# Token rows of six experts and of fifteen second-MLP tiles transposed through DRAM and VectorE instead of TensorE

## The chip, the cores and the metric

The kernel runs on one core of a Trainium2 chip. Its time is the device time of one execution in microseconds; the number compared is the median of several runs. A separate execution was recorded by the hardware profiler; times along the trace count from its first instruction.

## The reference

Three stages on 2304 tokens (4 batches of 576) of width 512. All inputs are float32.

```
q_s = softmax(q, over the 64 columns of a head)     # 8 heads
k_s = softmax(k, over the 576 rows)
x   = q_s @ (k_s^T @ v), heads side by side         # 2304 x 512

noisy = x @ w_gate + log1p(exp(x @ w_noise)) * noise   # 8 experts
top-2 of noisy per token, softmax over the two
x   = sum over the two experts e of weight * (relu(x @ w1[e]) @ w2[e])   # 512 -> 1024 -> 512

h   = x @ w_in                                       # 512 -> 1024
s   = h * softmax(h)
x   = (s - mean(s)) / sqrt(var(s) + 1e-6) * g_ln @ w_out   # 1024 -> 512
```

## The kernel before, in words

Matrix products that feed values into the two MLPs are done in three passes: each float32 operand is split into a high part (fp32r, made by a ScalarE copy) and a low part (the difference, made by VectorE), and TensorE adds high x high, high x low and low x high.

The order of the work is written out by hand; each engine takes its instructions in that order, and waits are placed where tiles are handed over or buffers are reused. DMAs are issued by SP, except the gathers, which POOL issues. SP issues in program order too: an issue that waits holds back all behind it.

**Attention and expert 0** follow a written-out list (ORDER) and take until about 180 us.

**Experts 1 to 7** are one loop. Each expert has room for 640 tokens, five tiles of 128. For an expert e, eight steps `mm1(e, m)` (L758) make a 128-row block of the hidden layer each; their results go through ScalarE (Relu, high part hh, L762) and VectorE (low part hl, L763), from two psum buffers in turn, so the matmuls of step m need the hl of step m - 2. In steps m < 4 the weights W2 of e are split and the weights W1 of e + 1 are loaded (`load_w1`, L148, one DMA of 512 KB). In steps m < 5 the token rows of e + 1 are gathered by POOL into a ring of five row tiles (`gather_x`, L727). From m = 3 on, one step of a background generator runs in each m: `decode_all`. Its first step only issues the loads of decode tiles 0 and 1 (`load_f64`, L195); after that a tile takes four steps of VectorE work (L203 to L218), the last of which also issues the store (L219) and the load of the tile two ahead. This generator makes w_in and w_out readable for the second MLP through DRAM copies win32 and wout32. Three decode buffers per tile come from a ring of four.

Then come five turns `mm2(e, a)` (L794), one per token tile, 24 matmuls each. In each turn the tile a of the next expert is transposed before them: `xt_tile` calls `transpose_split` (L734 four TensorE transposes into psum, L736 ScalarE copy to the high part, L737 VectorE subtraction to the low part). A turn also evacuates its result (L796, VectorE and ScalarE by turns) and stores it, does a decode step, splits a quarter of the next W1 and loads a quarter of the next W2.

**The second MLP** goes over 18 tiles. `gather_y` fetches the two expert results of a tile, `combine` weighs and adds them (L824, L825), `x2_trans` transposes the 128x512 result on TensorE and splits it (L734, L736, L737), `h_in` does 48 matmuls (L842), `solu` takes the row maximum (L851), the exponential (L854), and the normalised product d (L855 to L862), `rstd` the variance (L870 to L880). For tiles 2 to 15 d already goes through DRAM: `d_write`, then `d_read` with four DMAs that put 32-row blocks in place, and `d_back`: one VectorE transpose in blocks of 32x32 (L898), a ScalarE copy (L901), a VectorE subtraction (L902). Other tiles transpose d on TensorE (`d_trans`). `o_out` does 24 matmuls (L925). One turn i of the final loop has `h_in(i)`, then d back for i - 2, x2 for i + 1, `solu(i)`, `combine(i + 3)`, `rstd(i - 1)` and `o_out(i - 3)` (`o_out(i - 2)` in turns 2 and 3, none in turn 4).

A transpose in blocks of 32x32 leaves the 512 contraction rows in another order over the partitions than a full transpose; the weights must be loaded in the same order, as `load_w2` already does for w_out.

Of the kernel before, what the change touches and what calls it, by code (L numbers as in the profile page):

```python
# [8 lines left out]
F32 = mybir.dt.float32  # L9
F32R = mybir.dt.float32r  # L10
F16 = mybir.dt.float16
I32 = mybir.dt.int32
U32 = mybir.dt.uint32
# [12 lines left out]
NA = 5  # L26
# [27 lines left out]

NP = 2

ORDER = """
F:100011101100000000100000000000101111 lk:0 lq:0 lkl:0 lk:1 kr:0 kmt:0 qm:0 lvl:0 km:0:0 klt:0 kl:0 km:0:1 kb:0
lk:2 kr:1 qs:0 lv:0 rz:0 ks:0 kmt:1 ksl:0 qe:0 kr:2 km:1:0 T:0 kmt:2 rz:1 km:1:1 C:0 kb:1 lkl:1 rz:2 T:1 km:2:0
# [25 lines left out]
def attn_moe_kernel(ctx: ExitStack, tc: tile.TileContext, q, k, v, w_gate, w_noise, noise,  # L85
# [11 lines left out]
    def slot(tag, shape, dt, name):  # L97
        return sb.tile(shape, dt, tag=tag, name=name)

    def ring(*tags):  # L100
        state = [-1]

        def take(shape, dt, name):
            state[0] = (state[0] + 1) % len(tags)
            return slot(tags[state[0]], shape, dt, name)
        return take

    new_raw = ring("R2", "R3", "R0", "R1")
    new_row = ring("S0", "S2", "S4", "S1", "S3")
    new_out = ring("S9", "S8", "S10")  # L110
    new_s2 = ring("S5", "S6", "S7", "S11")
    psA = ctx.enter_context(tc.tile_pool(name="psA", bufs=2, space=PSUM))
    psB = ctx.enter_context(tc.tile_pool(name="psB", bufs=2, space=PSUM))
# [4 lines left out]
    tab = dram.tile([OVT * 128, 2], I32, name="tab")  # L118
    win32 = dram.tile([DM, FF], F32, name="win32")
    wout32 = dram.tile([FF, DM], F32, name="wout32")  # L120
    dd = {t: dram.tile([128, FF], F32, name=f"dd{t}") for t in range(NP, NC - 2)}

    def bank_t():
# [20 lines left out]

    def load_w1(e, j):
        t = new_raw([128, KD, 256], F32, "raw")
        src = win32 if e == E else w1[e]
        SP.dma_start(out=t, in_=src[:, 256 * j:256 * j + 256].rearrange("(k p) f -> p k f", p=128))  # L148
        raw[1, e, j] = t

    def load_w2(e, j):
# [46 lines left out]
    def decode(i):  # L198
        _, dst, rs, c0 = dec_src(i)
        t = d64.pop(i).rearrange("p (c w) -> p c w", w=2)  # L200
        lw, hw = t[:, :, 0], t[:, :, 1]
        a, b, c = (new_s2([128, 512], U32, f"dec{j}") for j in range(3))
        V.tensor_scalar(b, hw, 3, 0x3FFFFFF8, op0=OP.logical_shift_left, op1=OP.bitwise_and)  # L203
        V.scalar_tensor_tensor(a, hw, 0xC0000000, b, op0=OP.bitwise_and, op1=OP.bitwise_or)
        V.scalar_tensor_tensor(a, lw, 29, a, op0=OP.logical_shift_right, op1=OP.bitwise_or)
        yield

        V.tensor_scalar(b, lw, 0x1FFFFFFF, 6, op0=OP.bitwise_and, op1=OP.logical_shift_right)
        V.tensor_scalar(c, a, 0xFF800000, None, op0=OP.bitwise_and)
        V.tensor_tensor(b, b, c, op=OP.bitwise_or)  # L210
        yield
        af, bf, cf = (x.bitcast(F32) for x in (a, b, c))
        V.tensor_sub(bf, bf, cf)
        V.scalar_tensor_tensor(af, bf, 2.0 ** -23, af, op0=OP.mult, op1=OP.add)
        yield

        V.tensor_scalar(c, hw, 20, 0x7FF, op0=OP.logical_shift_right, op1=OP.bitwise_and)
        V.scalar_tensor_tensor(af, c, 896.5, af, op0=OP.is_ge, op1=OP.mult)  # L218
        SP.dma_start(out=dst[rs, c0:c0 + 512], in_=af)  # L219
# [501 lines left out]
    xg = {}  # L721

    def gather_x(e, a):
        t = new_row([128, DM], F32, "xg")
        c = E * a + e
        first = e == 0 and a < TA
        P.indirect_dma_start(out=t, out_offset=None, in_=xd[0:NRA, :] if first else xd, in_offset=bass.IndirectOffsetOnAxis(  # L727
            ap=idxA[:, a:a + 1] if first else idx[:, c:c + 1], axis=0))
        xg[e, a] = t

    def transpose_split(t, hi, lo):
        ps = bank_t()
        for kk in range(KD):
            T.transpose(ps[:, 128 * kk:128 * kk + 128], t[:, 128 * kk:128 * kk + 128], ident)  # L734
        pv = ps.rearrange("p (k t) -> p k t", k=KD)
        A.copy(hi, pv)  # L736
        V.tensor_sub(lo, pv, hi)  # L737
# [3 lines left out]
    def xt_tile(e, a):  # L741
        if a == 0:
            XT[e] = (slot("XH", [128, KD, CAP], F32R, "xh"), slot("XL", [128, KD, CAP], F32R, "xl"))
        hi, lo = XT[e]
        transpose_split(xg.pop((e, a)), hi[:, :, 128 * a:128 * a + 128], lo[:, :, 128 * a:128 * a + 128])

    hT = {}

# [72 lines left out]
    def combine(t):  # L821
        a, b = yg.pop((t, 0)), yg.pop((t, 1))
        c = col_of(t)
        A.activation(out=a, in_=a, func=AF.Copy, scale=gw[:, c, 0:1])  # L824
        V.scalar_tensor_tensor(a, b, gw[:, c, 1:2], a, op0=OP.mult, op1=OP.add)  # L825
        x2r[t] = a

    def x2_trans(t):
        a = x2r.pop(t)
# [14 lines left out]
                                 stop=(kk == KD - 1 and s == 2), skip_group_check=True)  # L844
        hb[t] = pa

    def solu(t):
        pa = hb.pop(t)
        c = col[:, t]
        pf = pa.rearrange("p n f -> p (n f)")  # L850
        V.reduce_max(c[:, 0:1], pf, axis=AX, negate=True)  # L851
        ed = new_ed([128, 2, FF], F32, "ed")
        e, d = ed[:, 0], ed[:, 1]
        A.activation(out=e, in_=pf, func=AF.Exp, bias=c[:, 0:1], accum_out=c[:, 1:2])  # L854
        V.tensor_scalar(c[:, 2:3], c[:, 1:2], 1e-9, None, op0=OP.add)  # L855
        V.reciprocal(c[:, 2:3], c[:, 2:3])
        V.scalar_tensor_tensor(d, pf, c[:, 2:3], e, op0=OP.mult, op1=OP.mult, accum_out=c[:, 3:4])  # L857
        V.tensor_scalar(c[:, 4:5], c[:, 3:4], -1.0 / FF, None, op0=OP.mult)
        if NP <= t < NC - 2:
            V.tensor_scalar(d, d, c[:, 4:5], None, op0=OP.add)  # L860
        else:
            V.tensor_scalar(e.rearrange("p (k g c) -> p g k c", g=4, k=KF), d.rearrange(  # L862
                "p (g k c) -> p g k c", g=4, k=KF), c[:, 4:5], None, op0=OP.add)
            e, d = d, e
        rsd[t] = e, d, c[:, 7:8]
# [23 lines left out]
    def d_read(t):  # L889
        x = dq[t] = new_dq([128, 2, FF], F32, "dq")  # L890
        for g in range(4):
            SP.dma_start(out=x[32 * g:32 * g + 32, 0].rearrange("i (b f) -> i b f", b=4),
                         in_=dd[t].rearrange("(b i) f -> i b f", i=32)[:, :, 256 * g:256 * g + 256])

    def d_back(t):
        x = dq.pop(t)
        xt = x[:, 1].rearrange("p (k b i) -> p k b i", k=KF, b=4)
        V.transpose(xt.rearrange("p k b i -> p b k i"), x[:, 0].rearrange("p (b k c) -> p b k c", b=4, k=KF))  # L898
        xt = xt.rearrange("p k b i -> p k (b i)")
        dt = new_dT([128, 2, KF, 128], F32R, "dT")  # L900
        A.copy(dt[:, 0], xt)  # L901
        V.tensor_sub(dt[:, 1], xt, dt[:, 0])  # L902
        dT[t] = (dt[:, 0], dt[:, 1])

    def d_trans(t):
        d = rsd[t][1]
# [222 lines left out]
    for e in range(1, E):  # L1129
        for m in range(KF):  # L1130
            mm1(e, m)
            if m < 4:
                split_w2(e, m)
                load_w1(e + 1, m)
            if e + 1 < E and m < NA:
                gather_x(e + 1, m)
            if m >= 3:
                next(bg, None)
            if e == 2 and m == 5:
                pair_gates()  # L1140
                count_overflow()
        if stop:
            return
        for a in range(NA):
            if e + 1 < E:
                xt_tile(e + 1, a)
            mm2(e, a)
            if e < E - 1:
                next(bg, None)
                if a < 4:  # L1150
                    split_w1(e + 1, a)
                    load_w2(e + 1, a)
                continue
            gather_y(a)
            if a < 2:
                for j in (2 * a, 2 * a + 1):
                    split_w1(E, j)
                    load_w2(E, j)
            elif a == 2:
                next(bg, None)  # L1160
                combine(0)
                split_w2(E, 0)
            elif a == 3:
                x2_trans(0)
                combine(1)
                split_w2(E, 1)
# [7 lines left out]
    for i in range(NC + 3):  # L1174
        if i < NC:
            h_in(i)
        if i == 1:
            d_trans(0)
        if NP <= i - 1 < NC - 2:
            d_read(i - 1)  # L1180
        if NP <= i - 2 < NC - 2:
            d_back(i - 2)
        if 2 <= i < NC - 1:
            x2_trans(i + 1)
        if i < NC:
            solu(i)
        if NP <= i < NC - 2:
            d_write(i)
        if i == 0:
            x2_trans(2)  # L1190
        if i < NC - 3:
            combine(i + 3)
        if i == 1:
            split_w2(E, 3)
        if 1 <= i <= NC:
            rstd(i - 1)
        if 2 <= i < 2 + NP:
            o_out(i - 2)
        if i >= 3 + NP:
            o_out(i - 3)  # L1200
        if i in (NP, NC - 1, NC):
            d_trans(i - 1)
        if i + 5 < NC:
            gather_y(i + 5)

# [30 lines left out]
```

## Time and profile before

| | us |
|---|---|
| median of 3 runs | 807.34 (806.57 to 809.58) |
| profiled execution | 807.68 |
| its span, first to last instruction | 806.0 |
| TensorE (matmul) busy | 758.2, 94% of the span |
| VectorE busy | 501.2, 62% |
| ScalarE busy | 293.8, 36% |
| GpSimd busy | 144.6, 18% |
| DMA moved | 119.98 MB, mean 149 GB/s |
| mean granted TensorE clock | 0.982 |

In the rows below PE is TensorE's matmuls, DVE VectorE, ACT ScalarE, POOL GpSimd and SPq the issue queue of SyncE. Matmul records overlap their neighbours: how far apart they start counts, not how long one is shown. An arrow names what ended a wait.

### The profile page before, as it was taken

Reading aid. Unit: us, or ns where it says so; the run is one execution under the profiler, and the core shown is the slowest. Engines: PE = TensorE matmul, PEld = TensorE weight load, DVE = VectorE, ACT = ScalarE, POOL = GpSimd, SP = SyncE. Lnnn points to the kernel's source line nnn. Section 1 sums busy time; section 2 is a strip of 40 time slices with the busy share of each in tenths; the row PEclk is TensorE's granted clock in tenths of the full one; section 3 lists DMA queues with packets and bytes.
Section 4 is the critical chain, followed back from the end, with each engine's and each line's share of the span. In section 5 each row is a group of like instructions: output and inputs, shape, how many; then the busy total and the mean of one; then the engine's idle time right before and its main releaser. Section 6 shows DMA issues by size and latency. Waiting matters only on the chain. (4 is left out here: it accounts for less than half of the span.)

```text
span 806.0 us, 12480 instructions
## 1 busy us (share of the span) xinstructions
PE 758.2 (94%) x4934; PEld 684.0 (85%) x4934; DVE 501.2 (62%) x884; ACT 293.8 (36%) x486; POOL 144.6 (18%) x130
## 2 busy tenths in 40 slices
PE   2877869999999999999999999999999999999997
PEld 1777867989789889889899899899898899989985
DVE  6998773334656656556556646546457767767661
ACT  1656531323223323223223232232345354444451
POOL 3684564020110110110200100000342111100000
PEclk9998888999999999999999999999999999999999
DMA  9973444265363454454543552432844545553311
GB/s 274 278 236 119 145 157 139 75 205 157 119 195 107 139 173 144 157 166 136 169 132 121 182 180 94 157 108 76 231 124 146 169 145 158 157 157 131 114 44 39
DMA packets 81534, 119.98 MB, mean 149 GB/s; under 512 B 14912, under 2 KB 52800, under 8 KB 81472
## 3 DMA queue, kind: packets, MB, share of 16 engines
q1 hardware_dynamic: 75392, 99.22, 38.6%
q0 software_dynamic: 6080, 19.93, 9.1%
q8 instruction: 39, 0.64, 0.3%
q14 instruction: 23, 0.19, 0.1%
HBM read 87.67 MB, written 31.46 MB: 148 GB/s over the span
## 5 line engine op out<-in xcount | busy, mean ns | idle before, releaser
L758 PE MATMUL a<-xh,w1h 128*128 128x320 f32 x448 | 138.5, 309 | 1.2 <-DVE hl L763 1.2
L758 PE MATMUL a<-xl,w1h 128*128 128x320 f32 x448 | 138.4, 309 | 0.0
L758 PE MATMUL a<-xh,w1l 128*128 128x320 f32 x448 | 138.3, 309 | 0.0
L794 PE MATMUL b<-w2h,hh 128*128 128x512 f32 x320 | 128.7, 402 | 0.0
L794 PE MATMUL b<-w2h,hl 128*128 128x512 f32 x320 | 126.7, 396 | 0.0
L794 PE MATMUL b<-w2l,hh 128*128 128x512 f32 x320 | 126.3, 395 | 0.0
L762 ACT ACTIVATE hh<-a 128x640 fp32r<-128x640 f32 x56 | 39.6, 707 | 159.8 <-PE a L758 159.8
L727 POOL DMA_INDIRECT xg<-xd,idx x38 | 40.7, 1071 | 304.1 <-PE t L734 294.3
L763 DVE SCALAR_TENSOR_TENSOR hl<-a,hh 128x640 fp32r<-128x640 f32 x56 | 46.1, 824 | 65.0 <-ACT hh L762 64.9
L758 PEld LDWEIGHTS a<-xh,w1h 128*128 128x128 f32 x448 | 84.2, 188 | 1.8 <-DVE hl L763 1.4
L758 PEld LDWEIGHTS a<-xl,w1h 128*128 128x128 f32 x448 | 84.1, 188 | 0.4
L758 PEld LDWEIGHTS a<-xh,w1l 128*128 128x128 f32 x448 | 84.2, 188 | 0.0
L817 POOL DMA_INDIRECT yg<-yd,posi x36 | 35.0, 973 | 208.6 <-DVE w1l L164 100.1
L794 PEld LDWEIGHTS b<-w2h,hl 128*128 128x128 f32 x320 | 60.0, 187 | 13.9
L794 PEld LDWEIGHTS b<-w2l,hh 128*128 128x128 f32 x320 | 60.2, 188 | 13.0
L794 PEld LDWEIGHTS b<-w2h,hh 128*128 128x128 f32 x320 | 60.2, 188 | 12.6
L164 DVE TENSOR_TENSOR w1l<-raw,w1h 128x1024 fp32r<-128x1024 f32 x32 | 38.9, 1222 | 33.4 <-ACT w1h L163 33.4
L842 PE MATMUL a<-w1h,x2h 128*128 128x256 f32 x288 | 57.5, 281 | 1.2 <-ACT x2h L736 0.7
L842 PE MATMUL a<-w1h,x2l 128*128 128x256 f32 x288 | 57.0, 279 | 0.0
L842 PE MATMUL a<-w1l,x2h 128*128 128x256 f32 x288 | 56.8, 278 | 0.0
L796 DVE COPY yo<-b 128x512 f32<-128x512 f32 x24 | 16.6, 692 | 64.2 <-PE b L794 64.2
L925 PE MATMUL b<-w2x,dT 128*128 128x512 f32 x216 | 54.3, 400 | 0.0
(209 smaller groups left out, 1399.3 us busy)
## 6 DMA issues: line engine op xcount, KB each, us to landing
raw<-in_moe_w_dram SPq DMA_DIRECT2D x64, 512.0 KB, 3.7
yd<-yo SPq DMA_DIRECT2D x40, 256.0 KB, 2.0
dd<-ed SPq DMA_DIRECT2D x14, 512.0 KB, 2.6
dq<-dd SPq DMA_DIRECT2D x56, 128.0 KB, 3.8
k<-in_k_dram SPq DMA_DIRECT2D x4, 1024.0 KB, 8.0
q<-in_q_dram SPq DMA_DIRECT2D x4, 1024.0 KB, 8.0
v<-in_v_dram SPq DMA_DIRECT2D x4, 1024.0 KB, 10.6
xd<-xr SPq DMA_DIRECT2D x8, 512.0 KB, 2.6
```

Of the source, the lines that this page charges most:

```text
L164: (pick_engine(20 + j, P, V) if e == 0 else V).tensor_sub(W1l[j], t, W1h[j])
L727: P.indirect_dma_start(out=t, out_offset=None, in_=xd[0:NRA, :] if first else xd, in_offset=bass.IndirectOffsetOnAxis(ap=idxA[:, a:a + 1] ...
L758: T.matmul(pa[:, n, 0:HC], lhsT=a, rhs=b, start=(kk == 0 and s == 0), stop=(kk == KD - 1 and s == 2))
L762: A.activation(out=h2, in_=pa[:, :, 0:HC], func=AF.Relu)
L763: V.scalar_tensor_tensor(l2, pa[:, :, 0:HC], 0.0, h2, op0=OP.max, op1=OP.subtract)
L794: T.matmul(pb, lhsT=x, rhs=y, start=(kk == 0 and s == 0), stop=(kk == KF - 1 and s == 2))
L796: (A.copy if a % 2 else V.tensor_copy)(t, pb)
L817: P.indirect_dma_start(out=r, out_offset=None, in_=yd[0:n, :], in_offset=bass.IndirectOffsetOnAxis(ap=posi[:, c, j:j + 1], axis=0))
L842: T.matmul(pa[:, n, 256 * c:256 * c + 256], lhsT=x[:, kk, :], rhs=w[2 * n + c][:, kk, :], start=(kk == 0 and s == 0 and c == 0), stop=(kk ...
L925: T.matmul(pb, lhsT=x[:, kk, :], rhs=w, start=(kk == 0 and s == 0), stop=(kk == KF - 1 and s == 2))
```

## The change

Token rows of experts 2 to 7 (EQ = 2) are gathered into a ring of three hop tiles, written to DRAM and read back by four DMAs of 128 runs of 512 bytes per 32 partitions; VectorE transposes them in 32x32 blocks, ScalarE copies the high part and VectorE subtracts for the low part. The weights W1 of experts 2 to 7 and of the second MLP are loaded in four pieces in the matching order of rows. In the second MLP tiles 3 to 17 go the same way; tiles 0 to 2 are copied once into the matching order by ScalarE and still transposed by TensorE. The decode buffers have fixed places: the result alternates between two tiles, the two others are one each. The low parts of d and of x2 move behind the row maximum, where the exponential runs on ScalarE; the VectorE transposes move to the end of a turn.

```diff
--- before.py
+++ after.py
@@ -53,6 +53,8 @@
     return [(0, 128, (2 * j + c // R) * S + c % R, R)]
 
 NP = 2
+
+EQ = 2
 
 ORDER = """
 F:100011101100000000100000000000101111 lk:0 lq:0 lkl:0 lk:1 kr:0 kmt:0 qm:0 lvl:0 km:0:0 klt:0 kl:0 km:0:1 kb:0
@@ -108,6 +110,7 @@
     new_raw = ring("R2", "R3", "R0", "R1")
     new_row = ring("S0", "S2", "S4", "S1", "S3")
     new_out = ring("S9", "S8", "S10")
+    new_hop = ring("RH0", "RH1", "RH2")
     new_s2 = ring("S5", "S6", "S7", "S11")
     psA = ctx.enter_context(tc.tile_pool(name="psA", bufs=2, space=PSUM))
     psB = ctx.enter_context(tc.tile_pool(name="psB", bufs=2, space=PSUM))
@@ -118,6 +121,8 @@
     tab = dram.tile([OVT * 128, 2], I32, name="tab")
     win32 = dram.tile([DM, FF], F32, name="win32")
     wout32 = dram.tile([FF, DM], F32, name="wout32")
+    xx = {t: dram.tile([128, DM], F32, name=f"xx{t}") for t in range(3, NC)}
+    xs_d = {(e, a): dram.tile([128, DM], F32, name=f"xs{e}_{a}") for e in range(EQ, E) for a in range(NA)}
     dd = {t: dram.tile([128, FF], F32, name=f"dd{t}") for t in range(NP, NC - 2)}
 
     def bank_t():
@@ -144,8 +149,12 @@
 
     def load_w1(e, j):
         t = new_raw([128, KD, 256], F32, "raw")
-        src = win32 if e == E else w1[e]
-        SP.dma_start(out=t, in_=src[:, 256 * j:256 * j + 256].rearrange("(k p) f -> p k f", p=128))
+        src = (win32 if e == E else w1[e])[:, 256 * j:256 * j + 256]
+        if e < EQ:
+            SP.dma_start(out=t, in_=src.rearrange("(k p) f -> p k f", p=128))
+        else:
+            for g in range(4):
+                SP.dma_start(out=t[32 * g:32 * g + 32], in_=src[128 * g:128 * g + 128].rearrange("(k c) f -> c k f", c=32))
         raw[1, e, j] = t
 
     def load_w2(e, j):
@@ -199,7 +208,7 @@
         _, dst, rs, c0 = dec_src(i)
         t = d64.pop(i).rearrange("p (c w) -> p c w", w=2)
         lw, hw = t[:, :, 0], t[:, :, 1]
-        a, b, c = (new_s2([128, 512], U32, f"dec{j}") for j in range(3))
+        a, b, c = (slot(tag, [128, 512], U32, f"dec{j}") for j, tag in enumerate((("S5", "S6")[i % 2], "S7", "S11")))
         V.tensor_scalar(b, hw, 3, 0x3FFFFFF8, op0=OP.logical_shift_left, op1=OP.bitwise_and)
         V.scalar_tensor_tensor(a, hw, 0xC0000000, b, op0=OP.bitwise_and, op1=OP.bitwise_or)
         V.scalar_tensor_tensor(a, lw, 29, a, op0=OP.logical_shift_right, op1=OP.bitwise_or)
@@ -721,12 +730,22 @@
     xg = {}
 
     def gather_x(e, a):
-        t = new_row([128, DM], F32, "xg")
         c = E * a + e
+        t = (new_row if e < EQ else new_hop)([128, DM], F32, "xg")
         first = e == 0 and a < TA
         P.indirect_dma_start(out=t, out_offset=None, in_=xd[0:NRA, :] if first else xd, in_offset=bass.IndirectOffsetOnAxis(
             ap=idxA[:, a:a + 1] if first else idx[:, c:c + 1], axis=0))
         xg[e, a] = t
+
+    def write_x(e, a):
+        SP.dma_start(out=xs_d[e, a], in_=xg[e, a])
+
+    def read_x(e, a):
+
+        t = xg[e, a] = new_row([128, DM], F32, "xg")
+        for g in range(4):
+            SP.dma_start(out=t[32 * g:32 * g + 32].rearrange("i (b f) -> i b f", b=4),
+                         in_=xs_d[e, a].rearrange("(b i) f -> i b f", i=32)[:, :, 128 * g:128 * g + 128])
 
     def transpose_split(t, hi, lo):
         ps = bank_t()
@@ -741,8 +760,16 @@
     def xt_tile(e, a):
         if a == 0:
             XT[e] = (slot("XH", [128, KD, CAP], F32R, "xh"), slot("XL", [128, KD, CAP], F32R, "xl"))
-        hi, lo = XT[e]
-        transpose_split(xg.pop((e, a)), hi[:, :, 128 * a:128 * a + 128], lo[:, :, 128 * a:128 * a + 128])
+        hi, lo = (x[:, :, 128 * a:128 * a + 128] for x in XT[e])
+        t = xg.pop((e, a))
+        if e < EQ:
+            transpose_split(t, hi, lo)
+            return
+        x = slot(("S12", "Gt")[a % 2], [128, KD, 4, 32], F32, "xt")
+        V.transpose(x.rearrange("p k b i -> p b k i"), t.rearrange("p (b k c) -> p b k c", b=4, k=KD))
+        x = x.rearrange("p k b i -> p k (b i)")
+        A.copy(hi, x)
+        V.tensor_sub(lo, x, hi)
 
     hT = {}
 
@@ -823,7 +850,32 @@
         c = col_of(t)
         A.activation(out=a, in_=a, func=AF.Copy, scale=gw[:, c, 0:1])
         V.scalar_tensor_tensor(a, b, gw[:, c, 1:2], a, op0=OP.mult, op1=OP.add)
-        x2r[t] = a
+        if t in xx:
+            SP.dma_start(out=xx[t], in_=a)
+            return
+        p = x2r[t] = slot(f"RH{t}", [128, DM], F32, "x2p")
+        A.copy(p.rearrange("p (k g c) -> p g k c", g=4, k=KD), a.rearrange("p (g k c) -> p g k c", g=4, k=KD))
+
+    def x2_read(t):
+        x = x2r[t] = new_raw([128, 2, DM], F32, "xq")
+        for g in range(4):
+            SP.dma_start(out=x[32 * g:32 * g + 32, 0].rearrange("i (b f) -> i b f", b=4),
+                         in_=xx[t].rearrange("(b i) f -> i b f", i=32)[:, :, 128 * g:128 * g + 128])
+
+    def x2_turn(t):
+        x = x2r.pop(t)
+        hi = new_s2([128, KD, 128], F32R, "x2h")
+        lo = new_s2([128, KD, 128], F32R, "x2l")
+        xt = x[:, 1].rearrange("p (k b i) -> p k b i", k=KD, b=4)
+        V.transpose(xt.rearrange("p k b i -> p b k i"), x[:, 0].rearrange("p (b k c) -> p b k c", b=4, k=KD))
+        xt = xt.rearrange("p k b i -> p k (b i)")
+        A.copy(hi, xt)
+        x2T[t] = (hi, lo, xt)
+
+    def x2_low(t):
+        hi, lo, xt = x2T[t]
+        V.tensor_sub(lo, xt, hi)
+        x2T[t] = (hi, lo)
 
     def x2_trans(t):
         a = x2r.pop(t)
@@ -844,14 +896,19 @@
                                  stop=(kk == KD - 1 and s == 2), skip_group_check=True)
         hb[t] = pa
 
-    def solu(t):
-        pa = hb.pop(t)
+    def solu_max(t):
+        pa = hb[t]
         c = col[:, t]
         pf = pa.rearrange("p n f -> p (n f)")
         V.reduce_max(c[:, 0:1], pf, axis=AX, negate=True)
         ed = new_ed([128, 2, FF], F32, "ed")
         e, d = ed[:, 0], ed[:, 1]
         A.activation(out=e, in_=pf, func=AF.Exp, bias=c[:, 0:1], accum_out=c[:, 1:2])
+        hb[t] = pf, e, d
+
+    def solu(t):
+        pf, e, d = hb.pop(t)
+        c = col[:, t]
         V.tensor_scalar(c[:, 2:3], c[:, 1:2], 1e-9, None, op0=OP.add)
         V.reciprocal(c[:, 2:3], c[:, 2:3])
         V.scalar_tensor_tensor(d, pf, c[:, 2:3], e, op0=OP.mult, op1=OP.mult, accum_out=c[:, 3:4])
@@ -892,15 +949,19 @@
             SP.dma_start(out=x[32 * g:32 * g + 32, 0].rearrange("i (b f) -> i b f", b=4),
                          in_=dd[t].rearrange("(b i) f -> i b f", i=32)[:, :, 256 * g:256 * g + 256])
 
-    def d_back(t):
+    def d_turn(t):
         x = dq.pop(t)
         xt = x[:, 1].rearrange("p (k b i) -> p k b i", k=KF, b=4)
         V.transpose(xt.rearrange("p k b i -> p b k i"), x[:, 0].rearrange("p (b k c) -> p b k c", b=4, k=KF))
         xt = xt.rearrange("p k b i -> p k (b i)")
         dt = new_dT([128, 2, KF, 128], F32R, "dT")
         A.copy(dt[:, 0], xt)
-        V.tensor_sub(dt[:, 1], xt, dt[:, 0])
-        dT[t] = (dt[:, 0], dt[:, 1])
+        dT[t] = (dt[:, 0], dt[:, 1], xt)
+
+    def d_low(t):
+        hi, lo, xt = dT[t]
+        V.tensor_sub(lo, xt, hi)
+        dT[t] = (hi, lo)
 
     def d_trans(t):
         d = rsd[t][1]
@@ -1134,6 +1195,11 @@
                 load_w1(e + 1, m)
             if e + 1 < E and m < NA:
                 gather_x(e + 1, m)
+            if EQ <= e + 1 < E:
+                if 1 <= m < NA + 1:
+                    write_x(e + 1, m - 1)
+                if 3 <= m:
+                    read_x(e + 1, m - 3)
             if m >= 3:
                 next(bg, None)
             if e == 2 and m == 5:
@@ -1178,10 +1244,14 @@
             d_trans(0)
         if NP <= i - 1 < NC - 2:
             d_read(i - 1)
+        if 1 <= i < NC - 2:
+            x2_read(i + 2)
+        if i < NC:
+            solu_max(i)
         if NP <= i - 2 < NC - 2:
-            d_back(i - 2)
+            d_low(i - 2)
         if 2 <= i < NC - 1:
-            x2_trans(i + 1)
+            x2_low(i + 1)
         if i < NC:
             solu(i)
         if NP <= i < NC - 2:
@@ -1200,6 +1270,10 @@
             o_out(i - 3)
         if i in (NP, NC - 1, NC):
             d_trans(i - 1)
+        if NP <= i - 1 < NC - 2:
+            d_turn(i - 1)
+        if 1 <= i < NC - 2:
+            x2_turn(i + 2)
         if i + 5 < NC:
             gather_y(i + 5)
```

## Rows read from the trace of the kernel before

**Rows 1.** Busy time by stretch: us, then PE, PEld, DVE, ACT, POOL; clock, DMA, GB/s.
```profile
300.00:400.00 100.00, 100.00 (x580) 91.19 (x579) 60.36 (x84) 30.96 (x42) 8.77 (x8) 1.00 0.46 146
680.00:740.00 60.00, 60.00 (x399) 54.69 (x399) 43.61 (x88) 28.88 (x56) 5.67 (x6) 1.00 0.46 140
```

**Rows 2.** Waits of PE after 200 us: us in total, times, longest.
```profile
PE a L758 <- DVE hl L763: 1.2, 1, 1.2
```

**Rows 3.** Timeline around two turns of expert stages: start us, length us.
```profile
406.31 0.60 PE L734 MATMUL t<-ident,xg 128*128 128x128 f32 x4
...
406.98 0.39 PE L794 MATMUL b<-w2l,hh 128*128 128x512 f32 x1
407.20 0.39 PE L794 MATMUL b<-w2h,hl 128*128 128x512 f32 x1
...
412.33 0.31 PE L758 MATMUL a<-xh,w1h 128*128 128x320 f32 x1
...
409.22 0.69 DVE L737 TENSOR_TENSOR xl<-t,xh 128x512 fp32r<-128x512 f32 x1
```

**Rows 4.** The chain that ended last, at the second MLP's start: start us, length us.
```profile
618.47 0.66 PE t L734 x4
...
624.67 5.57 PE a L842 x48
...
630.70 0.59 ACT x2h L736
...
631.34 6.16 PE a L842 x48
637.50 0.44 PE t L734 x4
```

**Rows 5.** VectorE by line, 640 to 760 us: busy us, mean ns, idle before.
```profile
L898 DVE STREAM_TRANSPOSE dq<-dq 128x1024 f32<-128x1024 f32 x11 | 13.7, 1246 | 0.6 <-issue 0.4
L902 DVE TENSOR_TENSOR dT<-dq,dT 128x1024 fp32r<-128x1024 f32 x11 | 13.5, 1226 | 12.3 <-ACT dT L901 12.3
...
L737 DVE TENSOR_TENSOR x2l<-t,x2h 128x512 fp32r<-128x512 f32 x11 | 7.5, 684 | 0.0
...
L855 DVE TENSOR_SCALAR col<-col 128x1 f32<-128x1 f32 x11 | 1.7, 154 | 14.0 <-ACT ed L854 14.0
```

**Rows 6.** Timeline of VectorE at the second MLP's start.
```profile
618.33 0.68 DVE L916 TENSOR_TENSOR dT<-t,dT 128x512 fp32r<-128x512 f32 x1
...
620.38 1.22 DVE L851 TENSOR_REDUCE col<-a 128x1 f32<-128x1024 f32 x1
...
627.34 0.16 DVE L880 TENSOR_TENSOR col<-col 128x1 f32<-128x1 f32 x1
```

**Rows 7.** Timeline of DMA issues on SP: the first decode loads, one weight load, one d_read.
```profile
194.90 0.97 SPq L195 DMA_DIRECT2D f<-in_moe_w_in_dram  x2
...
397.31 0.38 SPq L154 DMA_DIRECT2D raw<-in_moe_w_dram  x1
...
673.92 1.75 SPq L892 DMA_DIRECT2D dq<-dd  x4
```

**Rows 8.** Timeline of VectorE in expert 1: the first decode step and what follows.
```profile
200.59 0.43 DVE L203 TENSOR_SCALAR dec<-f 128x512 uint32<-128x512 uint32 x1 [3.95 <-DMA f<-in_moe_w_in_dram]
...
202.39 0.82 DVE L763 SCALAR_TENSOR_TENSOR hl<-a,hh 128x640 fp32r<-128x640 f32 x1
```

**Rows 9.** TensorE before 130 us by stretch: us, PE busy, granted clock, DMA, GB/s.
```profile
114.60:118.20 3.60, 2.02 (x26) 1.00 0.35 86
118.30:121.70 3.40, 0.13 (x6) 0.89 0.00 0
121.70:127.80 6.10, 6.09 (x38) 0.50 0.01 3
```

**Rows 10.** DMA issues of the second MLP: count, KB each, median us to landing.
```profile
dd<-ed SPq DMA_DIRECT2D x14, 512.0 KB, 2.6
dq<-dd SPq DMA_DIRECT2D x56, 128.0 KB, 3.8
```

## The prediction

> **What bounds the kernel now.** I read the busy time by stretch first. In an expert stretch (300 to 400 us) and in the second MLP (680 to 740 us) TensorE is busy for all of it at a granted clock of 1.00, while VectorE stands at 60% and 73% and the DMA engines at 46% [rows 1]. The reader is to see that no other engine is near its limit there. Next come the waits that end idle time of TensorE after 200 us: the largest is 1.2 us, before a matmul of L758, released by VectorE [rows 2]; three more, under 1 us each, lie at the start of the second MLP [rows 4]. So from 200 us on the time is the sum of what TensorE executes, and an instruction taken off it is worth its own length, as long as nothing new is late.
>
> **The change part by part.**
>
> Transposes of experts 2 to 7. Six experts of five tiles lose four TensorE transposes each: 30 groups. In the timeline a group starts at 406.31 and the second matmul after it at 406.98; matmuls there follow each other every 0.23 (406.98 to 407.20). A group thus takes 0.67 - 0.23 = 0.44 us [rows 3]. 30 x 0.44 = 13.2 us go.
>
> What takes their place is a gather into a hop tile, one write to DRAM, four reads, one VectorE transpose, a ScalarE copy and a VectorE subtraction. The transpose of 128x512 is not in the trace. Bounds: 0.62 (half of the 1246 ns for 128x1024) and 1.25 (all of it); I take 0.65, near the half, because the 1024-wide subtraction and the 512-wide one (1226 and 684 ns) scale so [rows 5]. This is hidden if the last tile is ready when the next expert's first matmul starts. Before, the last low part ended at 409.91 and the matmuls of L758 began at 412.33 [rows 3], 2.4 us later. The new order adds a transpose (0.65) and a wait for ScalarE's copy (0.59, the x2h copy of [rows 4]) behind the same VectorE work, and the matmul comes 0.44 earlier: about 0.7 us remain, 0.1 with a transpose of 1.25. The first half of the matmuls needs only columns of the first three tiles, which is further cover. I cost it at nothing; without cover it would be up to 6 x 1 us.
>
> The Trainium skill ("VectorE: DVE Perf Modes", section "Rules for kernel authors") speaks against this exchange: for a 128x128 transpose it says to use TensorE if PSUM will do as destination. By that rule these groups would stay and this gain would be zero. The rows that make TensorE the only full engine decide here.
>
> SP in expert 1. This is the price I expect. SP issues in program order, and the first two decode loads (L195) sit at m = 3 of expert 1, now behind new issues. The W1 load of that step becomes four pieces: four issues take 1.75, as those of d do, against 0.38 for one weight load, +1.37. The write of tile 2 adds 0.38 and the four reads of tile 0 add 1.75 [rows 7]. Together +3.5 us; from below, if issues take less, +2.5, and from above +4.5 with more traffic ahead. Before, the load was issued at 194.90 and VectorE waited for it until 200.59, with the hl operation of L763 queued behind the decode step, at 202.39 [rows 7, 8]. TensorE's 1.2 us wait is this very wait: its next psum buffer is freed by that hl. So the late load goes straight onto the path: +3.4 us, and TensorE then stands idle for 1.2 + 3.4 = 4.6 us. The trace shows what such a gap does: TensorE was nearly idle from 118.3 to 121.7, and from 121.7 to 127.8 the granted clock was 0.50 (the 1.2 GHz level); a stretch of 3.6 us from 114.6 on, in which it was busy for 2.0, kept 1.00 [rows 9]. Half speed over 6.1 us costs about 3.0; where the low stretch ends sooner, 1.5. I take 2.5. Together +5.9 us, once. Later decode loads are issued two decodes ahead of their use and keep their cover.
>
> The Trainium skill ("DMA: Bandwidth & Descriptors", section "Issuing engines are not separate DMA queues") calls the sequencer's time to initiate a DMA usually small relative to the DMA itself. Here four issues take 1.75 us and the load some 5.7. Taken as negligible, the 3.5 us vanish and the sum is 5.9 better; that is the second rival.
>
> Two decode tiles. They take away VectorE waits for decode stores. No wait of TensorE hangs on those: nothing gained, nothing lost.
>
> The second MLP. 15 groups (tiles 3 to 17) go, 0.44 each by the chain [rows 4]: 6.6 us if all show. The first three fall into the start, where VectorE is late, so I follow it tile by tile. At 618.47 the transposes took 0.66 because they waited for VectorE's evacuation (L916), whose first half ends about 618.4 and second at 619.01 [rows 4, 6]. Without them the output matmuls start some 1.1 us earlier, tile 4's input matmuls run from about 623.5 to 629.1. VectorE: transpose of tile 4 to 619.65, maximum of tile 3 from 619.6 (before: 620.38); from there to the end of L880 took 620.38 to 627.50, 7.1, so now 626.7; transposes of d 1.25 and of tile 5 0.65 to 628.6; maximum of tile 4 from 629.1 to 630.3; then the d low part 1.23 and only after it tile 5's low part 0.62, done at 632.1 [rows 5, 6]. Tile 5's input matmuls have no output matmuls ahead of them (there is none in that turn) and need this low part after four of 48. They end at 632.1 + 44/48 x 5.57 = 637.2, against 637.50 before [rows 4]. So the first three groups and the old waits there are worth only 0.3 us together: the old waits go, and the low part queued behind d's is what is late next, by some 2 us. From there 12 groups count in full: 5.3. Sum 5.6; bounds 4 (another microsecond late) and 8 (no such wait: 6.6 and the old waits).
>
> In the steady turns VectorE needs the 7.1 above, 0.6 by which two low parts (1.23 + 0.62) outlast the wait for the exponential (14.0 / 11 = 1.27), 1.25 and 0.65: 9.6 us [rows 5, 6]. TensorE's turn becomes 11.1 (5.57 and some 5.55). The low part of the next tile is ready 3.1 us after a turn's input matmuls, wanted 5.6 after. The wait for the ScalarE copy of d (12.3 / 11 = 1.1) is gone too, and this makes the room. The extra copies of tiles 0 to 2 on ScalarE (0.59 each by that row) lie where VectorE and TensorE have other work; uncovered they cost 1.8.
>
> Sum: -13.2 - 5.6 + 5.9 = -12.9. The profiled execution took 807.68 us (span 806.0), so 794.8; it lies 0.3 above the median of 807.34, so the median becomes 794.4.
>
> **Rivals.** (1) The gap in expert 1 forms but the clock holds: 2.5 less, 792. For it: the gap is dense work right before and after. Against it: the fall that the rows show followed a shorter gap, 3.4 us [rows 9].
> (2) The late load costs nothing, as pieces are issued faster or data come sooner: 788.5. Against it: all four issue rows are over 0.3 us each.
> (3) More waits: the last x tile of each expert late by 1 us and the copies uncovered, 6 + 1.8: 802. For it: only 0.7 us of cover.
> (4) Slower: d's reads land late in the second MLP. Their VectorE transpose now comes in the same turn as the read. From a d write (5.9 into VectorE's turn) to that transpose (7.7 into the next, 11.1 later) there are some 13 us; the write lands in 2.6, four issues take 1.75, the reads land in 3.8 [rows 7, 10], which leaves about 5. The change doubles the DMAs of a turn. Should the landing pass 9 us, each microsecond more is paid in some 13 turns; at 11 us that is 26 us: 820. It decides from 10 us on. Against it: DMA engines at 46% [rows 1].
> (5) The reads through DRAM are not used in time at all and tiles are waited for in each expert: about 807.
>
> **How the numbers follow.** Forecast 0.50, rival 1 0.15, rival 2 0.13, rival 3 0.12, rival 4 0.06, rival 5 0.04. The predicted time is the forecast's 794.4. The range runs from 788.5 (rival 2) to 800.5: the forecast with its upper bounds (1 for the load, 0.5 for the clock, 1.6 for the start) and part of rival 3. Differences under 0.5% (4 us) count as no change. Faster: forecast, rivals 1 and 2 and nearly all of rival 3, 0.91; within: 0.04; slower: 0.05.
>
> **What would show it.** Right: 30 and 15 groups of L734 gone, three left in the second MLP and ten in experts 0 and 1; the expert period shorter by 2.2 us; one TensorE gap of 4 to 5 us near 205, released by hl behind a decode step, and a granted clock of 0.50 after it; a wait of about 2 us before tile 5's input matmuls, then turns of 11.1. Wrong: no gap near 205, or matmuls of L758 that wait for x low parts in every expert, or VectorE transposes that wait for reads.

## The result and the profile after

The changed kernel takes 797.37 us (794.43 to 799.58, 4 runs) against 807.74 for the kernel before in the same comparison; the ratio is 0.9874 [0.9848, 0.9899]. It is faster by 1.3%, 10.4 us; the prediction had 794.4. The profiled execution took 799.58 us (span 797.8), 8.1 less than the profiled one of before.

In every profile the stages are read from the first matmul of each kind in the timeline of TensorE; "the third tile's output" is the first output matmul of the third tile, and the last stage but one ends where the last output matmul starts:

| stage, us | before | after | difference |
|---|---|---|---|
| to the first matmul of expert 1 | 177.3 | 177.8 | +0.5 |
| hidden matmuls of expert 1 | 30.0 | 38.0 | +8.0 |
| from there to the second MLP | 379.7 | 367.0 | -12.7 |
| second MLP to the third tile's output | 50.7 | 52.6 | +1.9 |
| from there to the last output matmul | 162.6 | 157.8 | -4.8 |
| after it | 5.6 | 4.6 | -1.0 |

The transposes that went are worth what was counted: 29 groups in the third row and 11 in the fifth, 0.44 us each (one more group lies in the second row, four in the fourth). Two stretches lost, the second row and the fourth. The -1.0 after the last output matmul is not the change's: two variants of the kernel before (the old wait, and the same two tiles, below) have 4.6 us there too.

Busy time by stretch, after (us, then PE, PEld, DVE, ACT, POOL, then clock, DMA share, GB/s), for [rows 1]:

```profile
300.00:400.00 100.00, 100.00 (x574) 91.53 (x573) 67.26 (x94) 31.10 (x42) 10.98 (x10) 1.00 0.70 210
670.00:730.00 60.00, 60.00 (x379) 53.88 (x379) 46.93 (x94) 29.90 (x55) 3.77 (x4) 1.00 0.60 185
```

TensorE is as full as before; the DMA engines went from 46% to 70% and 60%. The waits of TensorE from 130 us on (total, times, longest), for [rows 2]:

```profile
PE a L785 <- DVE hl L790: 6.9, 1, 6.9
PE a L894 <- DVE x2l L877: 2.5, 2, 2.2
```

TensorE in six stretches, after (us, PE busy, granted clock, DMA share, GB/s):

```profile
202.40:209.40 7.00, 0.22 (x2) 0.71 0.98 284
209.40:215.60 6.20, 6.12 (x23) 0.51 0.69 204
215.60:222.00 6.40, 6.40 (x30) 1.00 0.42 127
626.40:628.50 2.10, 0.15 (x2) 1.00 0.84 204
628.50:631.90 3.40, 3.20 (x15) 0.50 0.72 197
632.00:640.00 8.00, 8.00 (x51) 1.00 0.85 253
```

Both waits are near-idle stretches, and after each the granted clock is 0.5, the 1.2 GHz level. In expert 1 the 24 matmuls of m = 7 then take 6.2 us (209.47 to 215.66), where 24 at full clock take 3.5 (one every 0.147 us in the same line of the first experiment).

What made VectorE late in expert 1 is in the DMA issues of SP and in VectorE's own timeline, after; these answer to [rows 7, 8]:

```profile
195.03 1.74 SPq L157 DMA_DIRECT2D raw<-in_moe_w_dram  x4
196.86 1.64 SPq L741 DMA_DIRECT2D xs<-xg  x1
198.69 1.97 SPq L747 DMA_DIRECT2D xg<-xs  x4
200.70 0.90 SPq L204 DMA_DIRECT2D f<-in_moe_w_in_dram  x2
```
```profile
206.81 0.43 DVE L212 TENSOR_SCALAR dec<-f 128x512 uint32<-128x512 uint32 x1 [9.63 <-DMA f<-in_moe_w_in_dram]
...
208.60 0.81 DVE L790 SCALAR_TENSOR_TENSOR hl<-a,hh 128x640 fp32r<-128x640 f32 x1
```

The reader sees the decode load issue at 200.70, behind a four-piece W1 load, one tile write and four tile reads, VectorE wait for it until 206.81, and the hl on which TensorE waits come after it.

The end of an expert stage, after: VectorE's last transpose and last low part, and the first matmul that needs the tile, for [rows 3]:

```profile
297.68 0.71 DVE L769 STREAM_TRANSPOSE xt<-xg 128x512 f32<-128x512 f32 x1
299.08 0.69 DVE L772 TENSOR_TENSOR xl<-xt,xh 128x512 fp32r<-128x512 f32 x1 [0.69 <-ACT xh L771]
```
```profile
300.36 0.31 PE L785 MATMUL a<-xh,w1h 128*128 128x320 f32 x1
```

The low part ends at 299.77, 0.6 us before the matmul: TensorE does not wait. The chain that ended last, at the second MLP's start (start us, length us), for [rows 4]:

```profile
620.09 5.58 PE a L894 x48
...
625.69 1.22 DVE col L903
626.91 1.13 DVE dT L963
628.05 0.61 DVE x2l L877
...
628.70 6.89 PE a L894 x44
635.59 5.57 PE b L986 x24
641.16 5.55 PE a L894 x48
```

After tile 4's matmuls the chain leaves TensorE: maximum, d's low part, x2's low part, and only then tile 5; its 44 matmuls take 6.89 instead of 5.1 (44/48 of 5.57). From there on it is TensorE alone, in turns of 11.1 us. VectorE by line, 640 to 750 us (busy us, mean ns, idle before), for [rows 5]:

```profile
L903 DVE TENSOR_REDUCE col<-a 128x1 f32<-128x1024 f32 x10 | 12.2, 1224 | 17.8 <-PE a L894 17.8
L963 DVE TENSOR_TENSOR dT<-dq,dT 128x1024 fp32r<-128x1024 f32 x10 | 12.2, 1215 | 0.0
...
L870 DVE STREAM_TRANSPOSE xq<-xq 128x512 f32<-128x512 f32 x10 | 6.7, 669 | 0.0
```

Its waits for ScalarE's copy and for the exponential are gone; it now waits 1.8 us a turn for TensorE.

### The profile page after: what moved, and what is told of

Its sections match the earlier page's. It is cut to its first block, busy times and chain, and to the rows that moved or that the text cites. A ratio compares the mean times of both kernels' runs of the same rounds, so it can differ in the third digit from the quotient of the medians.

```text
span 797.8 us, 12649 instructions
## 1 busy us (share of the span) xinstructions
PE 743.6 (93%) x4754; PEld 670.1 (84%) x4754; DVE 532.2 (67%) x929; ACT 298.7 (37%) x489; POOL 144.8 (18%) x130
## 5 line engine op out<-in xcount | busy, mean ns | idle before, releaser
L821 PE MATMUL b<-w2h,hh 128*128 128x512 f32 x320 | 126.3, 395 | 0.0
L736 POOL DMA_INDIRECT xg<-xd,idx x38 | 39.5, 1040 | 327.7 <-DMA xs<-xg 317.7
L844 POOL DMA_INDIRECT yg<-yd,posi x36 | 36.6, 1017 | 166.1 <-DVE w1l L173 72.9
L771 ACT CAST xh<-xt 128x512 fp32r<-128x512 f32 x30 | 18.6, 621 | 94.5 <-DVE xt L769 94.5
L986 PE MATMUL b<-w2h,dT 128*128 128x512 f32 x144 | 48.0, 395 | 0.0
```

The lines of the kernel that those rows point to most:

```text
L771: A.copy(hi, x)
L821: T.matmul(pb, lhsT=x, rhs=y, start=(kk == 0 and s == 0), stop=(kk == KF - 1 and s == 2))
L844: P.indirect_dma_start(out=r, out_offset=None, in_=yd[0:n, :], in_offset=bass.IndirectOffsetOnAxis(ap=posi[:, c, j:j + 1], axis=0))
L986: T.matmul(pb, lhsT=x[:, kk, :], rhs=w, start=(kk == 0 and s == 0), stop=(kk == KF - 1 and s == 2))
```

## The experiments

Each median stands beside that of the kernel before in its own comparison.

**The decode loads ahead of everything.**

```diff
     bg = decode_all()
+    next(bg)
     for e in range(1, E):
...
-            if m >= 3:
+            if m >= 3 and (e, m) != (1, 3):
                 next(bg, None)
```

> The changed kernel with the first two decode loads issued ahead of the loop over experts instead of at m = 3 of expert 1. Theory A (the loss in expert 1 is the late load on SP and the clock that falls after it): the TensorE gap of 7.2 us near 202 goes altogether, the granted clock stays at 1.00 there, mm1 of m = 7 takes 3.5 instead of 6.2 us; 5.7 + 1.3 + 2.7 = 9.7 us less than the changed kernel's 797.4: 787.7. Rival B (the added traffic itself makes VectorE or TensorE wait in expert 1, whatever the place of the load): another gap of several us stays there, 794 to 798. Rival C (the gap goes, but the clock falls anyway): 790.5.

Measured: 789.41 us against 808.64, ratio 0.9757 [0.971, 0.9803]. TensorE in that stretch:

```profile
195.00:210.00 15.00, 15.00 (x98) 1.00 0.88 247
```

No gap, no fall, and the hidden matmuls of expert 1 take 28.2 us instead of 38.0: 9.8 us, where theory A had 9.7. The traffic is still there (DMA share 0.88), so rival B falls, and C with it. The total came out 1.7 above the 787.7; in the profile the stretch ahead of expert 1 was 1.6 us longer than in the changed kernel (179.4 against 177.8).

**Half of the cause: loads at m = 3, but ahead of that step's write and reads.**

```diff
+            if (e, m) == (1, 3):
+                next(bg)
             if EQ <= e + 1 < E:
...
-            if m >= 3:
+            if m >= 3 and (e, m) != (1, 3):
                 next(bg, None)
```

> The changed kernel with the first two decode loads still at m = 3 of expert 1, but ahead of that step's tile write and four tile reads; only the W1 load in four pieces stays ahead of them. Theory A (the delay is what SP issues ahead of the loads, each issue with its own time): the loads issue near 197 instead of 200.7, the TensorE gap is 7.1 - 3.8 = 3.3 us, and the clock falls for less than the 10.2 us that it fell for: 797.4 - 3.8 - 1.5 = 792. Rival B (the load lands when the DMA engines have worked off the tile traffic, whatever its place): gap 6 to 7 us, 797. Rival C (only the W1 pieces count): gap above 5 us.

Measured: 794.95 against 807.80, ratio 0.9844 [0.9814, 0.9874]; the hidden matmuls of expert 1 take 34.4 us. Issue times on SP and VectorE's wait:

```profile
195.12 1.74 SPq L157 DMA_DIRECT2D raw<-in_moe_w_dram  x4
196.90 2.23 SPq L204 DMA_DIRECT2D f<-in_moe_w_in_dram  x2
199.22 0.38 SPq L741 DMA_DIRECT2D xs<-xg  x1
```
```profile
204.74 0.43 DVE L212 TENSOR_SCALAR dec<-f 128x512 uint32<-128x512 uint32 x1 [7.47 <-DMA f<-in_moe_w_in_dram]
```

The load issues 3.8 us earlier, as expected, but lands only 2.1 earlier: it takes 7.8 us against 6.1 in the changed kernel and 5.7 before. TensorE's wait is 4.7 us, between theory A's 3.3 and rival B's 6 to 7, and a little under rival C's 5; the total, too, lies between A and B. From issue to VectorE's start, this variant and then the changed kernel (us, PE busy, granted clock, DMA share, GB/s):

```profile
196.90:204.74 7.84, 5.81 (x40) 1.00 0.87 258
```
```profile
200.70:206.81 6.11, 1.92 (x14) 0.87 0.90 262
```

The place in SP's order counts, then, but an issue does not bring its own fixed time along, as theory A had it: of the 1.7 us that the load takes longer, 1.3 is SP's time for the two issues (2.23 against 0.90). The share of the DMA engines does not tell the two cases apart (0.87 and 0.90), so traffic as the cause is not shown.

**Experts 3 to 7 only.** One constant: `EQ = 2` becomes `EQ = 3`, so expert 1 prepares no DRAM tiles.

> The changed kernel with DRAM tiles for experts 3 to 7 only (25 instead of 30), so that expert 1 issues no tile writes and reads and loads W1 in one piece. Theory A (SP issues ahead of the first decode load make the gap of expert 1): five groups of transposes come back, +2.2 us, and the gap of expert 1 returns to 1.2 us at a clock of 1.00, -8.4: 797.4 + 2.2 - 8.4 = 791.2. Rival B (the gap comes from traffic or waits of any expert that uses DRAM tiles): a gap moves to expert 2, 797 to 800.

Measured: 794.81 against 808.64, ratio 0.9817 [0.9789, 0.9845]. TensorE's wait for hl:

```profile
PE a L785 <- DVE hl L790: 1.2, 1, 1.2
```

That is the old 1.2 us, the stage is 30.0 us as before, and no such wait appears in expert 2. With five groups fewer it still is no slower than the changed kernel. Rival B falls. The total came out 3.6 above the 791.2, of which 1.4 is the stretch ahead of expert 1 (179.2 us, see below); another 2.2 is that the 8.4 was read in a profiled execution, 799.58, and taken off a median, 797.4.

**The old wait in the kernel before.** The edit of the first experiment in the kernel before.

> The kernel before with the first two decode loads ahead of the loop over experts. Theory A (its largest wait of TensorE, 1.2 us, is that load): 1.3 us less, 806.0 to 806.5, no wait for hl left. Rival (another wait follows at once): no difference, 807.5.

Measured: 805.58 against 808.64, ratio 0.9962 [0.9947, 0.9976]. The wait for hl is gone and the stage takes 28.5 us, 1.5 less, so theory A's wait is the right one. Of the rest of the 3.1 between the medians the profiles show only the 1.0 after the last output matmul, which is not this edit's.

**x2's low part ahead of d's.**

```diff
-        if NP <= i - 2 < NC - 2:
-            d_low(i - 2)
         if 2 <= i < NC - 1:
             x2_low(i + 1)
+        if NP <= i - 2 < NC - 2:
+            d_low(i - 2)
```

> The changed kernel with the two low parts of a turn exchanged: x2's low part first, then d's. Theory A (tile 5's input matmuls wait for x2's low part queued behind d's, and the clock falls after that gap): the gap near 626 shrinks by the 1.1 to 1.2 us of d's low part, from 2.2 to about 1.1, the clock holds 1.00 there and saves another 1.8: 797.4 - 2.9 = 794.5. Rival B (the gap is set by the late row maximum or by ScalarE's high part): the gap stays at 2.2, 797.4. Rival C (the gap shrinks but the clock still falls): 796.3. The gap of expert 1 stays in all cases.

Measured: 797.07 against 808.64, ratio 0.9851 [0.9804, 0.9897]. The totals alone show nothing: the stretch ahead of expert 1 came out 1.9 us longer in this profile. The stage itself shows it: 50.3 us instead of 52.6. The wait before tile 5 (us in total, times, longest), and the stretch behind it:

```profile
PE a L894 <- DVE x2l L877: 1.4, 1, 1.4
```
```profile
628.90:634.00 5.10, 5.10 (x44) 1.00 0.66 197
```

It shrinks to 1.4 us, the clock stays at 1.00, and 44 matmuls take 5.1 us. Rivals B and C fall.

**Both orders mended.** The early loads of the first experiment, and in the second MLP x2 ahead of d throughout:

```diff
+        if 1 <= i < NC - 2:
+            x2_read(i + 2)
         if NP <= i - 1 < NC - 2:
             d_read(i - 1)
-        if 1 <= i < NC - 2:
-            x2_read(i + 2)
+        if 4 <= i < NC - 1:
+            x2_low(i + 1)
         if i < NC:
             solu_max(i)
+        if 2 <= i < 4:
+            x2_low(i + 1)
         if NP <= i - 2 < NC - 2:
             d_low(i - 2)
-        if 2 <= i < NC - 1:
-            x2_low(i + 1)
...
+        if 1 <= i < NC - 2:
+            x2_turn(i + 2)
         if NP <= i - 1 < NC - 2:
             d_turn(i - 1)
-        if 1 <= i < NC - 2:
-            x2_turn(i + 2)
```

> The changed kernel with the early decode loads of the first experiment, and in the second MLP: x2 read and turned ahead of d, and from turn 4 on x2's low part ahead of the row maximum (in turns 2 and 3 behind it, as it is). Theory A (both TensorE gaps and the clock that falls after them are the losses, and both are matters of order): no gap over 1 us after tile 4's input matmuls, clock at 1.00 there, the stretch from the first input matmul to the third tile's output 52.6 -> about 48.7 us; 789.4 - 3.9 = 785.5. Rival (the order only moves the wait to d: its high part and transpose come later, and the output matmuls wait for them): the stretch stays at 50 to 52 us and turns grow past 11.15: 788 or more.

Measured: 784.98 us (784.17 to 786.82) against 807.82, ratio 0.9718 [0.9694, 0.9741]. It is the best version, 12.4 us below the changed kernel. TensorE where the two gaps were:

```profile
195.00:206.00 11.00, 11.00 (x75) 1.00 0.85 250
590.00:603.00 13.00, 12.69 (x85) 1.00 0.71 213
603.00:622.00 19.00, 18.84 (x129) 1.00 0.74 221
```

The second MLP's start takes 48.7 us, as theory A had it, and its rest 157.8 as in the changed kernel, so nothing moved to d.

**The second MLP alone.** `EQ = 8`: all experts on TensorE transposes.

> The changed kernel with all experts on TensorE transposes, the second MLP as changed. Theory A: the stretch from expert 1's matmuls to the second MLP is as before (30.0 and 379.7 us, the wait of 1.2 us there), the second MLP's start costs 52.6 instead of 50.7 us, its rest 157.8 instead of 162.6: 3.0 us less than before, 805.2 where before is 808.2. Rival B (the start's gap comes from traffic of the experts): start at 49 to 50 us, 802.

Measured: 803.36 against 807.82, ratio 0.994 [0.9921, 0.996]. Stages 30.5, 379.7, 52.4 and 157.8 us: the middle as before, the start of the second MLP as in the changed kernel. Rival B falls, though the total lies between the two. The wait there (this time ended by VectorE's next instruction) is the same with no expert's tile going through DRAM:

```profile
PE a L894 <- DVE col L912: 2.2, 1, 2.2
PE a L785 <- DVE hl L790: 1.7, 1, 1.7
```

**Low parts at once.** Each low part of the second MLP directly behind its ScalarE copy:

```diff
-        if NP <= i - 2 < NC - 2:
-            d_low(i - 2)
-        if 2 <= i < NC - 1:
-            x2_low(i + 1)
...
             d_turn(i - 1)
+            d_low(i - 1)
...
             x2_turn(i + 2)
+            x2_low(i + 2)
```

> The changed kernel with each low part of the second MLP right behind its transpose and ScalarE copy again, instead of behind the row maximum of the next turn. Theory A (moving them behind the maximum makes the room on VectorE that 11.1 us turns need): VectorE's turn is 7.1 + 1.25 + 1.1 (wait for the copy) + 1.23 + 0.67 + 0.65 (wait) + 0.68 = 12.7 us, TensorE follows it: 13 turns x 1.5 us more, 797.4 + 20 = 817, slower than before. Rival B (the VectorE queue has room enough either way): turns stay at 11.15, 797.4.

Measured: 817.43 against 807.82, ratio 1.0104 [1.0074, 1.0134], slower than before. VectorE by line, 650 to 770 us, and TensorE's waits:

```profile
L963 DVE TENSOR_TENSOR dT<-dq,dT 128x1024 fp32r<-128x1024 f32 x10 | 12.3, 1226 | 11.2 <-ACT dT L958 11.2
...
L877 DVE TENSOR_TENSOR x2l<-xq,x2h 128x512 fp32r<-128x512 f32 x10 | 6.9, 692 | 6.8 <-ACT x2h L872 6.8
```
```profile
PE a L894 <- ACT x2h L872: 13.1, 12, 3.6
```

VectorE waits 1.1 and 0.7 us a turn for ScalarE, its turn is 12.6 us (12.7 expected), and TensorE follows: the rest of the second MLP takes 173.5 instead of 157.8 us. So in the second MLP the transposes pay only because the low parts moved.

**The decode buffers from the ring of four.**

```diff
-        a, b, c = (slot(tag, [128, 512], U32, f"dec{j}") for j, tag in enumerate((("S5", "S6")[i % 2], "S7", "S11")))
+        a, b, c = (new_s2([128, 512], U32, f"dec{j}") for j in range(3))
```

> The changed kernel with the decode buffers from the ring of four again. Theory A (no wait of TensorE hangs on decode stores): no difference beyond the spread, 797.4. Rival B (with more on SP the stores finish later, and VectorE in waiting for them makes the hl of L790 late): 1 to 5 us slower, with waits of TensorE for hl in several experts.

Measured: 817.75 against 807.82, ratio 1.0117 [1.0091, 1.0142]. This is the largest surprise: 20 us slower than the changed kernel. TensorE's waits for hl from 130 us on, and one of them on SP and on VectorE:

```profile
PE a L785 <- DVE hl L790: 14.7, 3, 6.0
PE b L821 <- DVE hl L790: 5.9, 2, 4.1
```
```profile
318.53 1.20 SPq L741 DMA_DIRECT2D xs<-xg  x1
319.78 1.94 SPq L747 DMA_DIRECT2D xg<-xs  x4
321.82 0.46 SPq L228 DMA_DIRECT2D win<-dec  x1
```
```profile
325.33 0.50 DVE L212 TENSOR_SCALAR dec<-f 128x512 uint32<-128x512 uint32 x1 [6.51 <-DMA win<-dec]
```

VectorE had the result ready at 317.7, but its store stood behind a tile write and four reads and issued at 321.82. In the ring the next tile's first buffer is the one being stored, so VectorE waited 6.51 us for it, hl behind it, and TensorE behind hl; the granted clock was 0.50 from 328.1 to 334.0. Of the five waits in the rows (20.6 us) one, of 6.0, is that of the late load in expert 1; the other four (14.6 us) come behind a VectorE wait for such a store (in one of them the profile names tile reads that landed at 397.37, 0.1 us after the store), and with the falls of the clock after three of them they go with a stretch of experts that is 23.5 us longer than in the changed kernel (390.5 against 367.0). Rival B is right, and its size was far too small.

**The same two tiles in the kernel before.** The reverse edit in the kernel before.

> The kernel before with the decode buffers of the changed one (two alternating result tiles, two fixed ones). Theory A (the two tiles matter only where stores queue behind tile reads on SP): no difference, 807.8. Rival B (the ring of four costs the kernel before too, about as much as it costs the changed one): several us faster, 800 or less.

Measured: 807.00 against 807.80, ratio 0.9994 [0.9978, 1.0009]: no difference, as theory A had it. The tiles are worth nothing there and 20 us in the changed kernel.

## Why the prediction was right, and where it was off

The mechanism and both places of loss were right; the sum came out 3.0 us low in the median (4.8 against the profiled execution, -8.1 for -12.9), because each of the two losses was mis-sized by about 2.6 us in the profile. Both lie outside the bounds worked out for them: the late load cost 8.4 us, where 5.9 and the two upper bounds make 7.4, and the second MLP gained 2.9 (4.8 less 1.9), where the lower bound was 4. That the median is nearer than the profiled execution is luck: that execution was the slowest of the four.

- *Transposes of experts, -13.2.* Measured -12.7 for the 29 groups that lie in one stage, 0.44 each. The cover held: 0.6 us before the matmul (0.7 predicted), with a transpose of 0.70 instead of 0.65.
- *The late decode load, +5.9.* This term of the sum was mis-sized. Measured +8.0, or +8.4 when the one group of transposes in that stage is added back. The delay, counted from the first matmul of expert 1, came to 5.2 us instead of 3.5: SP needed 1.64 us for the tile write (0.38 predicted) and 2.0 for the reads (1.75 predicted), and the load then took 6.1 instead of 5.7. Why that write took so long is open. TensorE stood for 6.9 us, not 4.6. The cost of the clock, 2.5 predicted, was 2.7.
- *The second MLP's start.* The late low part of tile 5 was found at its place, 2.2 us (2.0 predicted). What the step left out is the clock, which fell and cost 1.8 us. The trace of before has a case near it that the working did not weigh, a near-idle stretch of 2.5 us with a fall behind it (us, PE busy, granted clock, DMA share, GB/s):

```profile
87.30:89.80 2.50, 0.19 (x2) 1.00 0.00 0
90.30:93.60 3.30, 3.30 (x27) 0.50 0.43 95
```

  The first stretch got 1.9 us longer where the working gives 0.7 shorter (0.3 to the end of tile 5's matmuls, and the next transposes). Most of the 0.8 that the clock does not explain is tile 4: counted from the first input matmul of the second MLP, its input matmuls started 0.5 us earlier than before, not 1.1.
- *The steady turns, -5.3 for 12 groups.* Measured -4.8 over 11 of them. VectorE's turn is 11.1 less 1.8 of waiting, 9.4 (9.6 predicted), and its transposes of d waited 0.5 us in ten turns together, so the reads land in time and rival 4 did not come up.
- *Two decode tiles, "nothing gained, nothing lost".* As a difference to the kernel before this is right. As an account of the change it is wrong: it names no cover that they provide, and they keep 20 us from being lost. The working asked what the edit removes in the kernel before and not what it holds off in the changed one.

Rivals 1 and 2 fell to the two trace rows at clock 0.5 and to the experiment with early loads; the uncovered x tiles of rival 3 and the waits in each expert of rival 5 did not appear: no wait for them stands among those of TensorE.

Both pages of the Trainium skill that were weighed gave the wrong sum here. "VectorE: DVE Perf Modes", section "Rules for kernel authors", would have kept the transposes on TensorE; with the orders mended, moving them is worth about 20 us (ratio 0.9718 to the kernel before, of which the early loads alone bring 0.9962). "DMA: Bandwidth & Descriptors", section "Issuing engines are not separate DMA queues", calls the issue time usually small; here the issues ahead of one load (1.74, 1.64 and 1.97 us) were most of the longest wait.

Left open: the stretch ahead of expert 1, which the edits leave as it was, took between 176.7 and 179.7 us in the twelve profiles, with more or fewer falls of the clock in its gaps. It may make much of the spread of the totals; that is not shown, as each kernel has one trace. Stages are therefore compared, not totals, where a few microseconds decide. Open too is why the clock fell after some waits of 2.2 us and not after others.

## What to carry to other kernels

Where TensorE is full and another engine has room, moving transposes off it pays their full length; what has to be looked for is a short-fused wait on the queues that the replacement uses. List every DMA that the new issues are put ahead of, and ask for each how soon after its issue it is needed: the first load of a pipeline, and a store whose buffer is the next to be written, have no slack, and an engine that runs in order passes their delay to work that has nothing to do with them. Then look at the buffers of every neighbour on that queue, and order the pieces of a turn by who is waited for first.

## What the runs showed of the hardware

- A wait of TensorE of 2.2 to 2.6 us at the start of the second MLP was followed by a granted clock of 0.50 in four profiles (628.5 to 631.9 in the changed kernel; the early loads, experts 3 to 7 only, the second MLP alone); waits of 2.1 and 2.2 us at the same place by none in two (loads ahead of the tile reads, ring of four); one of 1.4 us by none. The longer wait of 6.9 us in expert 1 was followed by 6.2 us of matmuls at 0.51, that of 4.7 us by 2.9 at 0.50.
- The time that SP needs for an issue is not fixed: a tile write took 0.38 us at one place and 1.64 at another, two decode loads 0.90 and 2.23. The share of the DMA engines does not tell the two writes apart: 0.85 during the one of 1.64 us, 0.88 during one of 0.38 (at 199.22 in the variant with loads ahead of the tile reads).
- One VectorE transpose of 128x512 in 32x32 blocks took 0.70 us in the experts and 0.67 in the second MLP, somewhat over half of the 1.25 for 128x1024.
